# Two block sizes from one gram of 96 columns, and a unit's VectorE work cut into pieces, in a woven RWKV6 and Mixer kernel

## Chip, cores and metric

One core of one Trainium2 chip. The metric is the device time in microseconds (us) of that core. Ratios are taken between runs of the same rounds on the same chip. Engines are written as the profile writes them: PE is TensorE's products, PEld its weight loads, DVE is VectorE, ACT is ScalarE, POOL is GpSimd. The words "issue" and "releaser" are the profile's: the releaser is what ended an idle stretch, and "issue" means that the engine waited for nothing that the profile shows.

## The reference

```python
B, H, S, D = 4, 8, 768, 48                 # batch, heads, tokens, head dim
state = zeros(B, H, D, D)
for t in range(S):                         # the recurrence, "attention" below
    cur = einsum('bhd,bhe->bhde', u * k[t], v[t])
    y[t] = einsum('bhd,bhde->bhe', r[t], state + cur)
    state = w[t][..., None] * state + einsum('bhd,bhe->bhde', k[t], v[t])
x = y as (B, S, H * D)                     # 384 wide
h = relu(x.T @ w_tok1) @ w_tok2            # token mixing, 256 wide
u = x + h.T
out = u + relu(u @ w_ch1) @ w_ch2          # channel mixing, 1536 wide
```

The kernel does the recurrence in chunks of 64 tokens. Within a chunk the weights of token on token are built up in levels: level l joins blocks of b = 2^l tokens in pairs, and needs the *gram* (the products of k with r) of each right block with its left one, multiplied by the decay between. A *unit* is 256 tokens of a batch with all heads: three units to a batch, twelve in all.

## The kernel before

PE is kept busy by mixing: while batch n is mixed, the three units of batch n + 1 are computed in between. `woven` decides what stands where: each list of pieces is spread evenly by the weights of its pieces, and the lists are merged. A weight is thus not a time that anything checks, only a share of the list.

```python
def woven(*lists):
    keyed = []
    for n, pieces in enumerate(lists):
        total, at = sum(c for c, _ in pieces), 0.0
        for i, (c, f) in enumerate(pieces):
            keyed.append(((at + c / 2) / total, n, i, c, f))
            at += c
    return [(c, f) for *_, c, f in sorted(keyed, key=lambda e: e[:3])]
```

The levels of a unit. A gram goes through four 64-row tiles of the array side by side (`fours`); a join is one or two multiplications on VectorE that bring r, k and the decays from one level to the next; a pick copies what is valid of a gram into the unit's weights, under a mask. From unit 6 on (`NEAR`) level 0 is not a gram but row sums on VectorE (`nearest`).

```python
def gram(l):                                   # level 1 to 4, one block size each
    b = 1 << l
    right = r_.rearrange("p (n two b) -> p n two b", two=2, b=b)[:, :, 1, :]
    g = L["g"] = ps_g.tile([128, 2, 512], f32, name="gram")
    for ca in range(UC * A):
        fours(lambda q, j, rows, cols: pe.matmul(
            g[cols, q, ts(ca, 32)], k_[rows, ds(ca * 128 + j * T, T)],
            right[rows, ts(2 * ca + j, 32 // b), :], start=True, stop=True))
...
def join(l, w, new):
    ...
    dve.tensor_mul(halves, halves, by)                           # r and k, 1024 elements a row
    dve.tensor_mul(new[:ROWS], wv[:, :, 0], wv[:, :, 1])         # the decays of the next level

def block(l):
    gram(l)
    join(l, products[l], products[l + 1])
    pick(l)
...
pieces = [(0.1, begin)] + ([(1.6, first_block)] if i < NEAR else [])
for l in range(1, LEVELS):
    pieces.append((1.2, lambda l=l: block(l)))
```

`beside` puts the end of one unit (`tokens`, `carry`, `update`, `before`, `within`: products with the state and the values) and the levels of the next unit into one list; `one` ties two groups of small products together, so that they come one behind the other. The last lines weave that list with the mixing of a batch. The z products (`up`) and q products (`down`) are the mixing's full-size ones; `turned` is the second half of token mixing with the transposes behind it.

```python
def beside(i, after, ahead):
    tokens, carry, update, before, within, *loads = after
    begin, *rest = ahead
    row0, row1, place = nearest(i + 1)
    ...
    return [(1.0, begin[1]), tokens, one(carry, rest[0]), update, one(before, rest[1]), one(within, rest[2]),
            *loads, *rest[3:], row0, row1, place]
...
for bt in range(B):
    ...
        hiddens, pieces, ups, downs = mixing(bt)
        pieces = [(3.9, lambda h=h: emit(h)) for h in hiddens] + pieces
        for s in range(S // SEG):
            pieces += ups[s] + downs[s]
    ...
        for i in range(n, n + UB):
            att += beside(i, post(i), levels(i + 1)) if i + 1 < NU else post(i)
        emit(woven(att, pieces))
```

## Time and profile before

| | before |
|---|---|
| time, median of 3 runs | 604.68 us (603.76 to 605.39) |
| span in the profile | 601.6 us |
| PE, PEld, DVE, ACT busy | 570.0, 486.6, 361.0, 177.1 us |
| loop: batch 0 mixed, units 3 to 5 between, from 138.5 us | 90.4 us, PE idle 3.5 |
| batch 1 mixed, units 6 to 8 between | 134.6 us, PE idle 0.3 |
| batch 2 mixed, units 9 to 11 between | 129.7 us, PE idle 0.05 |
| batch 3 mixed, nothing between | 105.2 us, PE idle 0 |

The lower four rows cut the span. ("The loop" is the first of these.) Where PE and PEld overlap, PE idle is the length less PE's busy time.

### The profile page before, as it was taken

Reading aid. Unit: us, or ns where it says so; the run is one execution under the profiler, and the core shown is the slowest. Engines: PE = TensorE matmul, PEld = TensorE weight load, DVE = VectorE, ACT = ScalarE, POOL = GpSimd, SP = SyncE. Lnnn points to the kernel's source line nnn. Section 1 sums busy time; section 2 is a strip of 40 time slices with the busy share of each in tenths; the row PEclk is TensorE's granted clock in tenths of the full one; section 3 lists DMA queues with packets and bytes.
Section 4 is the critical chain, followed back from the end, with each engine's and each line's share of the span. In section 5 each row is a group of like instructions: output and inputs, shape, how many; then the busy total and the mean of one; then the engine's idle time right before and its main releaser. Section 6 shows DMA issues by size and latency. Waiting matters only on the chain.

```text
span 601.6 us, 18874 instructions
## 1 busy us (share of the span) xinstructions
PE 570.0 (95%) x8596; PEld 486.6 (81%) x8596; DVE 361.0 (60%) x599; ACT 177.1 (29%) x428; POOL 7.2 (1%) x32
## 2 busy tenths in 40 slices
PE   3787899899999989999999999999999999999997
PEld 2776658776888886789989896789898986898987
DVE  5789699999675867666457376528446422040404
ACT  6155444422433313241141231231313312302020
POOL 4000000000000000000000000000000000000000
PEclk9997599999999999999999999999999999999999
DMA  8534564620233235141124103001200000000000
GB/s 340 195 83 152 163 199 151 208 70 28 82 110 109 67 82 158 29 133 28 53 57 132 28 28 106 2 2 43 65 2 28 2 27 0 1 20 8 27 2 27
DMA packets 22976, 45.85 MB, mean 76 GB/s; under 512 B 2512, under 2 KB 14928, under 8 KB 22896
## 3 DMA queue, kind: packets, MB, share of 16 engines
q1 hardware_dynamic: 22752, 44.64, 23.3%
q8 instruction: 67, 1.10, 0.8%
q14 instruction: 13, 0.11, 0.1%
q10 hardware_dynamic: 144, 0.00, 0.0%
HBM read 39.91 MB, written 4.72 MB: 74 GB/s over the span
## 4 chain that ended last, share of the span: by engine, by line
PE 79%; DVE 13%; DMA 3%; issue 3%; ACT 2%; SPq 0%; DVEq 0%; ACTq 0%
PE z_ps L554 29%; PE q_ps L588 24%; PE gram L307 7%; PE h_ps L534 4%; PE h_ps L527 4%; DVE rk L341 3%; DMA x<-in_w_ch_dram 2%; PE h_ps L564 2%; PE kv_ps L440 2%; PE y_ps L489 2%; PE y_ps L476 2%; PE gram L430 2%; DVE at L323 2%; PE xT_ps L546 1%; DVE scratch L218 1%
## 5 line engine op out<-in xcount | busy, mean ns | idle before, releaser
L554 PE MATMUL z_ps<-xT,wch 128*128 128x256 f32 x864 | 195.9, 382 | 1.6 <-ACT z L556 1.6
L554 PEld LDWEIGHTS z_ps<-xT,wch 128*128 128x128 f32 x864 | 161.0, 190 | 23.8 <-ACT z L556 2.8
L556 ACT ACTIVATE z<-z_ps 128x256 f32<-128x256 f32 x144 | 55.0, 382 | 171.3 <-PE z_ps L554 158.2
L588 PE MATMUL q_ps<-wch,z 128*128 128x192 f32 x528 | 94.6, 329 | 0.0
L588 PEld LDWEIGHTS q_ps<-wch,z 128*128 128x128 f32 x528 | 86.1, 190 | 1.4
L588 PE MATMUL q_ps<-scratch,z 128*128 128x192 f32 x396 | 70.0, 328 | 0.0
L307 PE MATMUL gram<-rk 48*64 48x32 f32 x3072 | 62.7, 234 | 6.6 <-issue 3.2
L307 PEld LDWEIGHTS gram<-rk 48*64 48x64 f32 x3072 | 58.2, 152 | 12.4 <-issue 6.4
L341 DVE TENSOR_TENSOR rk<-rk,decay 112x1024 f32<-112x1024 f32 x36 | 44.0, 1223 | 35.7 <-PE gram L307 26.1
L588 PEld LDWEIGHTS q_ps<-scratch,z 128*128 128x128 f32 x396 | 64.4, 190 | 0.4
L341 DVE TENSOR_TENSOR rk<-rk,w 112x1024 f32<-112x1024 f32 x36 | 44.0, 1223 | 28.9 <-PE gram L307 23.9
L580 DVE TENSOR_TENSOR z<-z 128x768 f32<-128x768 f32 x11 | 10.5, 957 | 65.6 <-ACT z L556 65.6
L527 PE MATMUL h_ps<-x,wtok 128*128 128x384 f32 x96 | 35.6, 518 | 0.0
L534 PE MATMUL h_ps<-h,wtok 128*128 128x384 f32 x96 | 35.3, 492 | 0.0
L323 DVE COPY_PREDICATED at<-mask,gram 128x512 f32<-128x512 uint8 x36 | 32.2, 895 | 0.0
L457 DVE TENSOR_TENSOR state<-state,kv_ps 128x192 f32<-128x192 f32 x40 | 14.2, 356 | 24.4 <-PE kv_ps L440 23.5
L331 ACT COPY at<-gram 16x256 f32<-16x256 f32 x48 | 17.4, 363 | 33.7 <-PE gram L307 32.5
L536 DVE TENSOR_TENSOR x<-x,h_ps 128x384 f32<-128x384 f32 x24 | 13.3, 553 | 23.1 <-PE h_ps L534 23.1
L527 PEld LDWEIGHTS h_ps<-x,wtok 128*128 128x128 f32 x96 | 18.5, 201 | 10.4 <-issue 0.6
L534 PEld LDWEIGHTS h_ps<-h,wtok 128*128 128x128 f32 x96 | 16.4, 190 | 9.6 <-ACT h L529 2.6
L431 ACT COPY kT<-gram 128x512 f32<-128x512 f32 x24 | 14.0, 585 | 28.5 <-PE gram L430 28.3
L318 ACT COPY at<-gram 32x256 f32<-32x256 f32 x48 | 17.4, 363 | 14.2 <-PE gram L301 13.7
(84 smaller groups left out, 514.9 us busy)
## 6 DMA issues: line engine op xcount, KB each, us to landing
rk<-in_rkw_dram SPq DMA_DIRECT2D x36, 192.0 KB, 3.4
x<-in_w_ch_dram SPq DMA_DIRECT2D x10, 512.0 KB, 4.3
vt<-in_v_dram SPq DMA_DIRECT2D x12, 384.0 KB, 4.4
out_dram<-o SPq DMA_DIRECT2D x24, 192.0 KB, 1.9
rp<-in_near_dram SPq DMA_DIRECT2D x12, 384.0 KB, 3.6
scratch<-in_w_ch_dram SPq DMA_DIRECT2D x8, 512.0 KB, 4.3
w<-in_rkw_dram SPq DMA_DIRECT2D x18, 192.0 KB, 3.2
rk<-in_rkw_dram SPq DMA_DIRECT2D x6, 512.0 KB, 6.5
```

What stands on the lines that cost most here:

```text
L307: fours(lambda q, j, rows, cols: pe.matmul(g[cols, q, ts(ca, 32)], k_[rows, ds(ca * 128 + j * T, T)], right[rows, ts(2 * ca + j, 32 // b), ...
L318: act.copy(at[p:p + b, :, ts(c, A), b:], g[ds(p + c * b, b)])
L323: dve.copy_predicated(out=dst, data=g.rearrange("p q (m b) -> p q m b", b=b), mask=masks[l].rearrange("p x t -> p (x t)").rearrange("p (m ...
L331: act.copy(at[p:p + b, :, :, n * 2 * b + b:(n + 1) * 2 * b], g[p:p + b, :, :, ts(n, b)])
L341: dve.tensor_mul(halves, halves, by)
L431: act.copy(L["kT"][:, c], ps)
L457: dve.tensor_add(new, new, got)
L527: pe.matmul(sums[i], wtok1[:, c, ts(i, 128)], xs[bt][:, c, :], start=(c == 0), stop=(c == C - 1))
L534: pe.matmul(ps, wtok2[:, i, ts(c, 128)], h1[:, i, :], start=(i == 0), stop=(i == DTOK // 128 - 1))
L554: pe.matmul(ps, wch1[:, m, ts(jt, 128)], xT[:, m, ts(s, SEG)], start=(m == 0), stop=(m == DM // 128 - 1))
L556: act.activation(zs[s][:, jt, :], ps, AF.Relu)
L588: pe.matmul(ps, a[:, j, :], b[:, j, :], start=(j == 0), stop=(j == HJ - 1))
```

## The change

The intent: from batch 2's units on (unit 6 and later) two levels share one gram. Each group of four blocks b needs six block columns: the right neighbour of a pair (level l) and, for level l + 1, the r of blocks 2 and 3 brought forward past blocks 1 and 2. Those 32 + 64 = 96 columns are laid out first (`spread`), one gram of 96 columns replaces two of 32, and three picks of 3b, 2b and b columns take it apart. VectorE pays with more and smaller operations. Because these would hold up the mixing's own VectorE work, they become pieces of their own, with weights of their own.

```diff
+        def spread(l, c):
+            ...
+            late(newest(act), act, copies)                       # two copies on ScalarE
+            dve.tensor_mul(y[:, :, 1:5:3], of[:, :, 2:4], ...)
+            dve.tensor_mul(y[:, :, 2], y[:, :, 4], ...)
+        def gram4(l):
+            for c in range(UC):
+                g = L["g", c] = ps_g.tile([128, 2, 512], f32, name="gram")
+                for a in range(A):
+                    fours(lambda q, j, rows, cols: pe.matmul(
+                        g[cols, q, ts(a, 96)], k_[rows, ds((c * A + a) * 128 + j * T, T)],
+                        L["far", c][rows, ts(2 * a + j, 96)], start=True, stop=True))
+        ... join_k, join_r, pick4 (three predicated copies a half unit)
+        if i >= NEAR:
+            return pieces + [(c, lambda f=f, a=a: f(*a)) for l in (1, 3) for c, f, a in (
+                (0.9, spread, (l, 0)), (0.9, spread, (l, 1)), (1.5, gram4, (l,)), (1.5, join_k, (l,)), (1.5, join_r, (l,)),
+                (1.4, pick4, (l, 0)), (1.4, pick4, (l, 1)))] + [(0.9, lambda: block(5))]
...
-        return [(0.3, lambda c=c: late(newest(dve), dve, lambda: row(c))) for c in range(UC)] + [
-            (0.2, lambda: (place(), load_near(i + 1)))]
+        return [(x, lambda c=c, n=n: late(newest(dve), dve, lambda: row(c, n)))
+                for c in range(UC) for n, x in enumerate((1.0, 0.6, 1.0))] + [(2.0, place)]
...
+        return [(2.0, begin[1]), far0, far1, tokens, one(carry, gram), join_k, join_r, loads[2], later0, pick0, loads[3], later1,
+                pick1, one(before, gram_), join_k_, join_r_, (0.01, lambda: load_near(i + 1)), pick0_, pick1_,
+                one(within, last), *loads[:2], *ends]
```

(`loads[2]` and `loads[3]` are the two halves of the state's update.) The list of a near unit now weighs 34.2 where it weighed 12.2, while the lists of earlier units keep their weights.

## The prediction

> **What bounds the kernel now.** I read the page's slices first, then busy time by stretch, then the groups, then TensorE's timeline around a few groups. The slices show who is full.
>
> ```profile
> PE   3787899899999989999999999999999999999997
> PEld 2776658776888886789989896789898986898987
> DVE  5789699999675867666457376528446422040404
> ```
>
> From the tenth slice on TensorE (PE) is at 9 nearly everywhere, while VectorE (DVE) falls from 9 to between 2 and 7. A busy PE alone proves little, so I cut the span at the starts of the three later batches (the first token-mixing products of L527, at 228.86, 363.44 and 493.10 us in the chain of waits) and at the start of the loop that mixes batch 0 with the attention of batch 1 (138.5 us).
>
> ```profile
> 138.50:228.86 90.36, 86.89 (x2294) 75.68 (x2294) 66.31 (x114) 29.59 (x77) 0.33 (x3) 1.00 0.28 82
> 228.86:363.44 134.58, 134.24 (x2064) 116.66 (x2063) 84.92 (x148) 36.50 (x92) 0.22 (x2) 1.00 0.24 71
> 363.44:493.10 129.66, 129.61 (x1743) 112.12 (x1743) 66.65 (x123) 32.47 (x81) 0.00 (x0) 1.00 0.10 31
> 493.10:598.34 105.24, 105.23 (x534) 92.42 (x533) 24.54 (x45) 18.60 (x47) 0.00 (x0) 1.00 0.03 10
> ```
>
> Columns: stretch, length, then busy us of PE, PEld, DVE, ACT, POOL, granted clock, DMA. The last batch is mixing alone, 105.2 us. Batch 1 has the same mixing plus three units of attention: 134.6 - 105.2 = 29.4 us. A unit's own products are tokens 0.9, carry, before and within 0.97 each, five grams 4.85 (below), together some 8.7 us, and 0.2 us lost at each return to full-size products makes it 9.7; three units are 29. So that stretch is the sum of its products: **no wait is left in it to win, only product time.** The same holds for batch 2 (two units' levels, three units' ends). Only the loop before, 138.5 to 228.86, has idle: 90.36 - 86.89 = 3.5 us plus about 2 us of slow stretches inside busy groups.
>
> The part that the change touches is the grams:
>
> ```profile
> L307 PE MATMUL gram<-rk 48*64 48x32 f32 x3072 | 62.7, 234 | 6.6 <-issue 3.2
> L341 DVE TENSOR_TENSOR rk<-rk,decay 112x1024 f32<-112x1024 f32 x36 | 44.0, 1223 | 35.7 <-PE gram L307 26.1
> L323 DVE COPY_PREDICATED at<-mask,gram 128x512 f32<-128x512 uint8 x36 | 32.2, 895 | 0.0
> ```
>
> 3072 records are 12 units x 4 levels x 32 products x 2 records. The mean of 234 ns is latency; the rate comes from the timeline, start to start:
>
> ```profile
> 293.70 1.10 PE L307 MATMUL gram<-rk 48*64 48x32 f32 x64
> 294.73 6.74 PE L554 MATMUL z_ps<-xT,wch 128*128 128x256 f32 x30
> 301.40 1.15 PE L489 MATMUL y_ps<-vt,at 64*64 64x48 f32 x64
> 302.37 1.10 PE L307 MATMUL gram<-rk 48*64 48x32 f32 x64
> 303.40 5.45 PE L554 MATMUL z_ps<-xT,wch 128*128 128x256 f32 x24
> 308.78 1.14 PE L307 MATMUL gram<-rk 48*64 48x32 f32 x64
> ```
>
> A level of 32 columns takes 1.03 us behind a group of the same tiling (302.37 to 303.40), 1.06 alone; 64 records of 48 columns take 0.97 (301.40 to 302.37). So 15 to 16.6 ns a record, whatever the columns. In the timeline the 64-column gram of the earlier units (L284) also takes 1.06. The z products run at 215.8 ns a record (15.54 us for 72 in the last batch's chain), so 30 should take 6.47 and take 6.67: 0.2 us goes at each return from small tiles.
>
> **What the Trainium skill says.** "TensorEngine Tiling (Array Packing)", Instruction Overhead, says that a product of 1 column has the latency of one of 60. The trace agrees in kind: 32, 48 and 64 columns cost the same. Key Properties there says that changing the tiling mode drains the array; the 0.2 us agrees in kind. "VectorE: DVE Perf Modes", the errata section, gives (N+151)/0.96 ns for a float32 tensor-tensor operation; the trace has 354 ns at 192, 553 at 384, 953 at 768 and 1223 at 1024, which is the same line to 1%, so I use it (via the trace) for sizes not seen. "Perfetto Trace Analysis", Identifying the Most-Contended Engine, warns that matmul occupancy overstates; hence the sum above.
>
> **The change part by part**, for units 6 to 11 (six of twelve).
>
> TensorE. Now, levels 1 to 5: 1.04 + 1.03 + 1.03 + 1.06 + 0.69 = 4.85 us a unit. After: two grams of 64 records with 96 columns stand for levels 1 to 4, and level 5 stays (0.69). The full array needs 215.8/256 = 0.84 ns a column, so 96 columns stream in 81 ns; four tiles side by side make 20.2 ns a record. At 64 columns that bound is 13.5 and 16.5 was seen, so the bound begins to bind between; I take 21.5 ns (an estimate), 1.38 us a gram. Then 2 x 1.38 + 0.69 = 3.45, **1.40 less.** Small groups: before carry, before and within each carry a gram, and levels 4 and 5 stand alone (five returns); after there are three returns. Two fewer, some 0.15 to 0.2 each: 0.3. Sum 1.7 us a unit, **10.2 us in six.** All is on the path, since batches 1 and 2 are sums of products; only unit 6, in the loop before, is less sure.
>
> VectorE. Now a unit's joins are 6 x 1.223 + 1.97 (decay products, 0.68 + 0.42 + 0.29 + 0.22 + 0.18 + 0.17) = 9.30 and its picks 1.29 + 0.70 + 0.70 = 2.69 (the 1.29 is level 1, runs of two): 12.0. After: join 0, 1.91; four spreads of 256 and 128 elements, 4 x (0.42 + 0.29) = 2.84; k joins 1.53 and 1.33; r joins 1.40 and 1.30; twelve predicated copies of 384, 256, 128 elements at 0.085 + 1.2 ns an element (from 0.70 at 512 and 1.31 at 1024), 1.18 per half unit, with a surcharge for short runs at level 1, together 5.4 (estimate); last join 1.40. Sum 17.1: **5.1 more a unit, 31 in all**, VectorE from 361 to about 392 us. ScalarE loses four copies of 0.363 (level 4) and gets eight of about 0.4 to 0.45: 2 us more a unit. All this lies beside TensorE: batch 1's VectorE goes from 85 to about 100 of some 129 us, the loop before from 66 to 72 of some 89.
>
> Order. The new piece weights (34 a unit instead of 12) squeeze units 3 to 5 into the first half of the loop before (33.7 of 67.9, formerly 33.7 of 46), and unit 11's end into the last 6% of batch 2. The first makes the join-gram chain of those units tighter, perhaps 2 us of new waits, though batch 1's first products are then free to fill in early; the second costs under 1 us, as each piece still has a product of 1.95 us behind it. Splitting updates and row sums costs nothing and lets additions of q products in between. Building the masks is a few small operations once.
>
> Sum: 604.7 - 10.2 + about 2 (loop before, net) + about 0.5 (VectorE in batches 1 and 2, mostly hidden) - 0.5 (two returns unit 6 or waits in its grams saved) = **596.5 us**, 1.4% less.
>
> **Rivals.** (1) VectorE becomes the bound in the quarter-product stretches. There mixing alone takes 6.7 of 13.65 us of VectorE, and attention adds about 10 of what is then some 17 us: full. Each q product needs an addition before its accumulator is free. Against it: in the stretches of z products there is no mixing work on VectorE, and finer pieces were made for just this. If it holds, 1 us is lost in each of some six such stretches and the pace of the loop before slips: 601 to 606. (2) The four tiles don't stream 96 columns side by side, say two share a path: 40 ns a record, 2.6 us a gram, the gain gone: 605 to 608. Against it: 64 columns at 16.5 ns would then be 27. (3) Both gram buffers are held from the gram to the picks, some 7 to 10 us, just where batches 1 and 2 turn their activations through the same buffers: up to 2 us each, 598 to 601. Against: the token-mixing back products need no such buffer. (4) The looser order also removes the 5 us of waits in the loop before: 590 to 592.
>
> **Range and chances.** The product term is 8 to 11 us; the waits between -4 and +7. Hence 591 to 602.5 in 8 of 10. The 2% line is 592.6, which needs full product gain and rival 4: 0.15. Slower than 616.8 needs rivals 1 and 2 together: 0.03. Within 2%: 0.82.
>
> **What would show it.** Right: 96-column gram groups of 64 records in 1.3 to 1.45 us start to start; 768 of them in all; 32-column records of L307 halved to 1536; batch 1 about 129.5 us and batch 2 about 126; VectorE 385 to 397 us busy; three returns a unit. Wrong: PE idle in batch 1 above 2 us with VectorE additions or gram buffers as the releaser (rivals 1, 3), 25 ns or more a record (rival 2), or the loop before longer than 90 us.

## The result, and the profile after

| | before | after |
|---|---|---|
| median of 6 runs each | 603.88 us (602.67 to 605.39) | 610.77 us (608.01 to 615.58) |
| ratio of the fast runs, 95% interval | | 1.0118 (1.0078 to 1.0158) |
| span in the profile | 601.6 | 609.0 |
| loop, PE idle | 90.2, 3.5 | 101.1, 8.2 |
| batch 1, PE idle | 134.6, 0.3 | 133.2, 2.5 |
| batch 2, PE idle | 129.7, 0.05 | 128.6, 1.8 |

A ratio here and below is the mean time of one kernel's fast runs over the mean of the other's fast runs of the same rounds, so it is not quite the ratio of the medians quoted. The change costs 1.2%: within 2% of before, yet well outside the range that was predicted, and on the wrong side. (The stage lengths are cut at the first product of each stage in the trace, hence 90.2 for the loop before where the prediction's window has 90.4.)

The slices after. PE has an 8 in slices 11, 13 and 15 where it had 9, and the granted clock (PEclk, tenths of full speed) drops to 7 and 8 in slices 12 and 13:

```profile
PE   3787799999898989999999999999999999999997
DVE  5789699999764798876639677727584351040403
PEclk9999699999978999999999999999999999999999
```

The stages (columns as in the prediction: stretch, length, busy us of PE, PEld, DVE, ACT, POOL, clock, DMA):

```profile
137.31:238.43 101.12, 92.92 (x2169) 80.51 (x2169) 75.44 (x143) 31.04 (x83) 2.70 (x17) 0.93 0.26 75
238.43:371.61 133.18, 130.72 (x1680) 113.15 (x1679) 96.09 (x213) 37.64 (x101) 0.22 (x2) 1.00 0.25 71
371.61:500.22 128.61, 126.84 (x1489) 109.69 (x1487) 73.06 (x161) 32.26 (x86) 0.00 (x0) 1.00 0.09 29
```

The loop got 10.9 us longer, at a mean clock of 0.93. Batches 1 and 2 each got a little over a microsecond shorter: PE's busy time there fell by 3.5 and 2.8 us, but idle time that was not there before took 2.1 and 1.7 of it back. The groups of the grams (L308 here is the line that is L307 in before):

```profile
L308 PE MATMUL gram<-rk 48*64 48x32 f32 x1536 | 38.4, 257 | 8.8 <-issue 5.7
...
L410 DVE COPY_PREDICATED at<-mask,gram 128x384 f32<-128x384 uint8 (+2 forms) x72 | 34.5, 482 | 14.4 <-PE gram L384 13.7
```

As many grams as predicted have gone: 1536 records of 32 columns remain (and 768 of 96 columns stand for the rest). From start to start in the trace, 64 of the new records take 1.45 us, 22.7 ns a record. In batch 1 the grams' time from start to start fell from 12.60 to 8.71 us. VectorE is at 386.2 us.

So where did the loop's 10.9 us go? PE's timeline in its middle, before, and after. (Columns: start us, busy us, engine, line, operation, tiles, count of records, and in brackets the idle time ahead with its releaser. A product of the program makes two records; the counts of products that are read from traces below are records.)

```profile
189.31 1.13 PE L307 MATMUL gram<-rk 48*64 48x32 f32 x64
190.37 2.86 PE L554 MATMUL z_ps<-xT,wch 128*128 128x256 f32 x12
193.16 1.15 PE L489 MATMUL y_ps<-vt,at 64*64 64x48 f32 x64
194.13 1.10 PE L307 MATMUL gram<-rk 48*64 48x32 f32 x64
```

```profile
188.98 1.15 PE L561 MATMUL y_ps<-state,rk 48*64 48x48 f32 x64 [0.45 <-DVE state L542]
189.92 0.88 PE L308 MATMUL gram<-rk 48*64 48x32 f32 x45
192.79 0.74 PE L308 MATMUL gram<-rk 48*64 48x32 f32 x18 [1.99 <-issue]
193.25 0.32 PE L574 MATMUL y_ps<-vt,at 64*64 64x48 f32 x2
```

In the kernel before, twelve full-size products (2.8 us) stand between two pairs of small groups. After, nothing does: state products, gram, value products and gram follow one another, 256 small products in a row, and after 109 of them PE stands still for 1.99 us with no releaser that the profile shows. The same happens at 166.32 us (1.50 us). The waits of PE in the loop (us in total, times, longest):

```profile
PE gram L308 <- issue: 3.5, 2, 2.0
PE q_ps L674 <- DVE o L688: 2.1, 1, 2.1
PE y_ps L561 <- DVE state L542: 1.2, 2, 0.8
```

Behind each of the two stops the granted clock is half for 6.8 us (168.9 to 175.75 and 192.8 to 199.6). That half clock costs more than the stop: where PE is the bound, 6.8 us at half speed do 3.4 us of work (an estimate; a gram of 64 products at half clock, from 170.56 us, took 1.86 us instead of 1.06). The sum for the loop: 4.7 us more idle, 2 x 3.4 from the clock, less some 1.5 that unit 6's new grams save, +10.0 of the +10.9 seen. (Before, no half clock falls in the loop. Both kernels have some ahead of it: before from 54.0 to 74.5 us, after from 66.5 to 76.8.)

Why a stop with no releaser? The trace records the fetches of instructions, as packets of 16,384 bytes. Before, the page counts 67 of them with 1.10 MB, and after, 61 with 1.00 MB. PE and PEld records times 64 bytes give 17,192 x 64 = 1.10 MB and 15,656 x 64 = 1.00 MB. So nearly all these packets are TensorE's, at 64 bytes an instruction: one packet holds 256 instructions, 128 pairs of weight load and product. At 16.5 ns a small product it lasts 2.1 us. The stop at 166.32 us ended 1.3 us after a packet had come in at 166.5 us, that at 190.80 us 1.7 us after one at 191.06. "Runtime: NRT & Kernel Launch", Instruction fetch mechanics, of the Trainium skill describes such fetches (blocks of 16 KiB, 256 instructions) and calls the cost of crossing a block "mostly hidden". The theory, then: **a long run of small products uses instructions up faster than they come.** It had to be tested, as "issue" only says what the profile does not show.

### The profile page after: what moved, and what is told of

It is laid out like the page before. It is cut to its first block, busy times and chain, and to the rows that moved or that the text cites. A ratio compares the mean times of both kernels' runs of the same rounds, so it can differ in the third digit from the quotient of the medians.

```text
span 609.0 us, 17474 instructions
## 1 busy us (share of the span) xinstructions
PE 568.1 (93%) x7828; PEld 484.6 (80%) x7828; DVE 386.2 (63%) x729; ACT 180.9 (30%) x452; POOL 9.6 (2%) x46
## 4 chain that ended last, share of the span: by engine, by line
PE 76%; DVE 14%; issue 4%; ACT 3%; DMA 2%; SPq 0%; DVEq 0%; ACTq 0%
PE z_ps L640 26%; PE q_ps L674 22%; PE h_ps L613 5%; PE h_ps L620 4%; PE gram L308 4%; PE kv_ps L522 2%; PE y_ps L574 2%; PE y_ps L561 2%; PE gram L512 2%; DVE at L410 2%; DVE rk L342 2%; PE h_ps L650 2%; PE xT_ps L632 1%; PE gram L384 1%; DVE state L542 1%
## 5 line engine op out<-in xcount | busy, mean ns | idle before, releaser
L674 PE MATMUL q_ps<-wch,z 128*128 128x192 f32 x528 | 94.6, 330 | 0.2 <-DVE z L700 0.2
L674 PEld LDWEIGHTS q_ps<-wch,z 128*128 128x128 f32 x528 | 87.6, 192 | 1.4 <-DVE z L700 0.5
L674 PE MATMUL q_ps<-scratch,z 128*128 128x192 f32 x396 | 71.9, 334 | 2.9 <-DVE o L688 2.9
L674 PEld LDWEIGHTS q_ps<-scratch,z 128*128 128x128 f32 x396 | 65.4, 193 | 4.2 <-DVE o L688 3.5
L308 PE MATMUL gram<-rk 48*64 48x32 f32 x1536 | 38.4, 257 | 8.8 <-issue 5.7
L308 PEld LDWEIGHTS gram<-rk 48*64 48x64 f32 x1536 | 35.7, 178 | 13.5 <-issue 6.7
L342 DVE TENSOR_TENSOR rk<-rk,decay 112x1024 f32<-112x1024 f32 x24 | 29.4, 1223 | 24.9 <-PE gram L302 15.5
L410 DVE COPY_PREDICATED at<-mask,gram 128x384 f32<-128x384 uint8 (+2 forms) x72 | 34.5, 482 | 14.4 <-PE gram L384 13.7
L342 DVE TENSOR_TENSOR rk<-rk,w 112x1024 f32<-112x1024 f32 x24 | 29.4, 1225 | 9.7 <-PE gram L308 7.4
L613 PEld LDWEIGHTS h_ps<-x,wtok 128*128 128x128 f32 x96 | 18.4, 199 | 10.9 <-issue 0.6
L622 DVE TENSOR_TENSOR x<-x,h_ps 128x384 f32<-128x384 f32 x24 | 13.3, 555 | 20.9 <-PE h_ps L620 20.9
L542 DVE TENSOR_TENSOR state<-state,kv_ps 128x192 f32<-128x192 f32 x40 | 14.1, 352 | 18.0 <-PE kv_ps L522 17.2
L633 ACT COPY xT<-xT_ps 128x384 f32<-128x384 f32 x24 | 11.5, 478 | 35.6 <-PE xT_ps L632 35.6
L512 PE MATMUL gram<-ident,rk 128*128 128x128 f32 x96 | 17.6, 311 | 3.8 <-ACT kT L513 3.1
```

Of the source, the lines that this page charges most:

```text
L308: fours(lambda q, j, rows, cols: pe.matmul(g[cols, q, ts(ca, 32)], k_[rows, ds(ca * 128 + j * T, T)], right[rows, ts(2 * ca + j, 32 // b), ...
L410: dve.copy_predicated(out=to[:, :, :, (q + 1) * b:], data=got[:, :, :, first * b:first * b + n], mask=masks4[l][:, q].unsqueeze(1).unsquee ...
L512: pe.transpose(ps[:, a, :], k_[:, ts(c * A + a, 128)], ident)
L542: dve.tensor_add(new, new, got)
L613: pe.matmul(sums[i], wtok1[:, c, ts(i, 128)], xs[bt][:, c, :], start=(c == 0), stop=(c == C - 1))
L622: dve.tensor_add(x[:, c, :], x[:, c, :], ps)
```

## The experiments

Three questions: what lengthens the loop, where the saving in batches 1 and 2 went, and whether both can be had. The theories at the start, in words: that the *order* made by the new weights (small products bunched, so that instructions run out and the clock falls) costs the loop's 10.9 us; against it, that *VectorE's added work* fills it (the prediction's first rival), or that the *grain of the pieces* does.

### e1_weights: the old weight for the new list

```diff
-        return [(2.0, begin[1]), far0, far1, tokens, ...]
+        near = [(2.0, begin[1]), far0, far1, tokens, ...]
+        return [(c * 0.36, f) for c, f in near]
```

The list weighs 12.3, close to the 12.2 of before the change; the work is that of after, to the instruction.

> The changed kernel with one edit: every weight of a near unit's list times 0.36, so that the list weighs 12.3 as before and units 3 to 5 are spread over the loop before batch 1 as in the kernel before. Theory A (the weave squeezed units 3 to 5, two groups of 256 small records came without a mixing product between, TensorE stood still there and its clock then fell to half): no half clock after 77 us, the loop from 137 us to batch 1's first L613 product falls from 101 to 89-91 us, the whole to 598-602. Rival B (VectorE's extra work in unit 6 and after is what costs): the loop stays above 97 us and the whole above 607. The rest (batches 1 and 2) should stay within 1 us of 133 and 128.5 us by both.

Measured 603.33 us against 604.47 for before, ratio 0.9988 (0.9966 to 1.0010).

```profile
139.90:230.40 90.50, 86.75 (x2165) 75.61 (x2165) 72.42 (x140) 31.45 (x83) 2.69 (x17) 0.98 0.31 84
230.40:363.60 133.20, 130.73 (x1680) 113.17 (x1679) 97.23 (x215) 37.70 (x101) 0.22 (x2) 1.00 0.25 71
```

The loop is back at 90.5 us from 101.1, with idle 3.8 instead of 8.2, and the half clock is down to one stretch of 3.4 us (behind a stop in unit 6's second gram, see e9). VectorE does the same work. So the loop's loss is the weights'. Batch 1 is as after, 133.2: its waits have another cause.

### e2_before_heavy: the new weight in the kernel before

```diff
-        return [(1.0, begin[1]), tokens, ...]
+        pieces = [(1.0, begin[1]), tokens, ...]
+        return [(c * (2.78 if i + 1 >= NEAR else 1.0), f) for c, f in pieces]
```

> The kernel before with one edit: the weights of the lists that hold a near unit's levels times 2.78, so that units 3 to 5 are squeezed as in the changed kernel, but every gram, join and pick is the old one. Theory A: the same two groups of 256 small records, gaps of 1.5 us or more in them, two stretches at half clock near 169 and 193 us, the loop from 138 us to batch 1 grows from 90 to 97-101 us, the whole to 610-614. Rival B (the new VectorE work is the cause): 603-606, no half clock after 75 us.

Measured 616.81 us, ratio 1.0184 (1.0144 to 1.0225).

```profile
138.30:242.00 103.70, 95.63 (x2298) 83.18 (x2298) 71.69 (x119) 30.56 (x79) 0.34 (x3) 0.92 0.28 78
```

```profile
PE gram L307 <- issue: 6.0, 4, 2.0
```

The loop takes 103.7 us with none of the change's work in it: only the weight differs. Four stops with "issue" as the releaser, of 1.49, 1.99, 0.65 and 1.92 us, and behind three of them half clock of 3.4, 6.8 and 6.8 us. Together with e1 this settles the first question: the order does it, in either kernel, and the grams of 96 columns are not needed for it.

### e4_coarse: two-size grams in coarse pieces with the old weights

```diff
+        def group(weight, *pieces):
+            return (weight, lambda: [f() for _, f in pieces])
+        return [(1.0, begin[1]), group(0.6, far0, far1), tokens, (2.3, one(carry, gram)[1]), group(1.2, join_k, join_r, pick0, pick1), ...]
```

> The changed kernel with the pieces joined again (k join, r join and both picks as one; both updates as one; row sums as two) and the old list weights, so the two-size gram alone, without the fine pieces. If the fine pieces are what keeps VectorE out of the way of the q products, this is 3-8 us slower than the changed kernel with its weights scaled (602-608); if the pieces' size matters little, it is within 2 us of it (597-603).

Measured 607.09 us, ratio 1.0037 (1.0010 to 1.0064). Loop 91.8, batches 1 and 2 together 261.5 us, where e1 with fine pieces has 261.9. So in batches 1 and 2 the grain makes no difference. The whole time is another matter: it is 3.8 us above e1's, which is the 602 to 608 expected if the fine pieces matter. The profiled run, the fastest of the four (604.46 us), had one stop of 1.95 us at 166.63 us in the loop and half clock behind it; the other three (607.03 to 607.62) have no profile. The list also weighs 13.4 here by its pieces, not 12.2. Whether the many small pieces, the second part of the change's idea, buy anything in the loop is therefore not shown.

### e3_dense and e11_wide: a run of small products by itself

Into the last batch, which has no attention, 16 extra grams whose results nobody uses: eight back to back (512 products), eight singly, each between pieces of six z products.

```diff
+                if bt == B - 1 and s == 1:
+                    more = ups[s][:6] + [(0.01, lambda: [small() for _ in range(8)])] + ups[s][6:]
+                if bt == B - 1 and s == 2:
+                    more = [e for f in ups[s] for e in (f, (0.01, small))][:16] + ups[s][8:]
```

> The kernel before plus 16 gram groups (64 records each, results unused) in the last batch, where nothing but TensorE limits: eight of them in one piece of 512 records, eight each behind three z products. Their operands are long ready and no reader waits. If fetching instructions limits dense small products (rival to a wait on VectorE), the 512 records show gaps of 0.5-2 us each ended by no engine, near the landings of instruction packets, and take 10-16 us instead of 8.5, while the spaced groups show none; perhaps half clock follows. If the gaps in the changed kernel came from VectorE alone, the 512 records take 8.3-8.6 us.

Correct, 629.14 us. The dense run:

```profile
547.88 2.99 PE L647 MATMUL gram<-rk 48*64 48x32 f32 x189
552.32 2.07 PE L647 MATMUL gram<-rk 48*64 48x32 f32 x128 [1.45 <-issue]
556.07 5.88 PE L647 MATMUL gram<-rk 48*64 48x32 f32 x195 [1.68 <-issue]
561.87 1.65 PE L554 MATMUL z_ps<-xT,wch 128*128 128x256 f32 x3
```

No reader waits and the operands are long ready, and yet PE stops after 189 products, and again after exactly 128 more, one packet's worth. The packets of instructions began to come at 549.93, 553.39, 557.45 and 561.52 us, 3.5 to 4.1 us apart, and each was in some 1 us later. Other transfers cannot have held them up much: the DMA engines were 2% busy. 512 products took 13.99 us instead of the 8.5 that eight single grams (1.06 us each, no stop) add up to, and the clock was half from 554.3 to 564.5 us, so that the last 195 took 30 ns each without a stop. Still it could have been the tiles, or having no reader. So e11 runs the same count with 192 columns, which stream more slowly:

```diff
-                pe.matmul(g[ts(j, T), q, ts(ca, 32)], k_[...], r_[rows, ds(ca * 128 + j * T, 32)],
+                pe.matmul(g[ts(j, T), q, ts(ca % 2, 192)], k_[...], r_[rows, ds(ca // 2 * 192, 192)],
```

> The same 16 added groups as in e3, each record with 192 instead of 32 columns: as many instructions, but 40 ns or more of streaming a record, so a packet of 256 instructions lasts some 5 us instead of 2. If it is the supply of instructions that fails in dense small products, the 512 records now run without gaps of 0.5 us or more (in e3 two of 1.5 and 1.7 us), in 20.5-23 us, and at full clock. If small tiles themselves, or the missing reader, stop TensorE, the gaps stay.

```profile
548.78 21.03 PE L647 MATMUL gram<-rk 48*64 48x192 f32 x512
569.74 2.42 PE L554 MATMUL z_ps<-xT,wch 128*128 128x256 f32 x10
```

Again one look, correct, 649.27 us. 512 products in one piece, 20.96 us (40.9 ns each), full clock, no stop; the packets came 4.8 to 5.4 us apart, as they were used up. Same tiles, same count, no readers: it is the rate of instructions that stops PE. Shown: the supply keeps up with a product in 40.9 ns and not with one in 16.5. Where between them it gives out was not measured; in all fifteen traces no two of these packets begin less than 3.3 us apart, which for 128 products is 26 ns each (an estimate). In the nine stops of this kind of 1.4 us and more (after, e2, e3, e4, e8), PE went on 2.4 to 2.9 us after a packet began to come, where 128 small products last 2.1 us. How long a run may be before it stops is not one number: 189 products here, 109 in the kernel after.

### e7_few_picks: VectorE relieved, with a wrong result

The second question. In batches 1 and 2 PE now stands idle with VectorE as the releaser. The waits of PE in batch 1 of the kernel after:

```profile
PE xT_ps L632 <- DVE x L622: 0.8, 1, 0.8
PE q_ps L674 <- DVE o L688: 0.8, 1, 0.8
PE z_ps L640 <- DVE o L712: 0.4, 1, 0.4
PE xT_ps L632 <- DVE at L410: 0.3, 1, 0.3
```

Either VectorE has too much to do, or the mixing's additions (L622, L688, L712) stand behind the wrong things in its queue. Dropping two of three predicated copies tells these apart.

```diff
-            for q, first in enumerate((0, 3, 5)):
+            for q, first in enumerate((0,)):
```

> e1 with two of the three predicated copies of each pick left out: a wrong result on purpose. The order on TensorE is that of e1; VectorE loses 4 x (0.43 + 0.43) = 3.4 us a unit and is near the load of the kernel before. Theory C: TensorE's waits in batches 1 and 2 fall from 2.4 and 1.2 us to under 1 and 0.6, batch 1 to 130.5-132 us, batch 2 to 127-128, the whole to 599-601.5. If VectorE's added work doesn't matter, all stays within 0.5 us of e1 (603).

Measured 600.52 us, ratio 0.9942 (0.9903 to 0.9980), result wrong as meant.

```profile
226.80:360.10 133.30, 130.87 (x1679) 113.36 (x1679) 91.98 (x192) 37.74 (x101) 0.22 (x2) 1.00 0.25 71
```

VectorE does 5.2 us less in batch 1 (91.98 against e1's 97.23), and batch 1 takes 133.3 us against 133.2, batch 2 128.5 against 128.7. So the amount of work is not what makes batches 1 and 2 wait, as far as this cut reaches: 91.98 us is still above the 84.9 of before. This went against the expectation that load was the cause. The time gained lies in the loop (88.7 against 90.5), where a stop of 1.26 us and the half clock of e1 are gone (see e9).

### e5_sparse_q, e6_sparse_qt: attention kept away from the mixing's VectorE stretches

If the place in the queue is the cause, e1's own queue must show it. VectorE ahead of the addition that PE's transposes wait for:

```profile
240.36 0.36 DVE L539 COPY state<-kv_ps 128x192 f32<-128x192 f32 x1 [1.27 <-PE kv_ps L522]
...
243.50 0.95 DVE L393 TENSOR_TENSOR rk<-rk,decay 112x768 f32<-112x768 f32 x1
244.37 0.41 DVE L410 COPY_PREDICATED at<-mask,gram 128x128 f32<-128x128 uint8 x1
244.60 0.57 DVE L622 TENSOR_TENSOR x<-x,h_ps 128x384 f32<-128x384 f32 x1
```

VectorE itself stood idle for 1.27 us until the carry's products were there, then ran 4.2 us of attention work, and only then came L622; PE had waited 0.82 us for it. VectorE takes its pieces in the order of its queue here, so a piece that waits for PE holds up all behind it. The cure is another weave: give the mixing's pieces a smaller weight where they need VectorE, and fewer attention pieces fall there.

```diff
+            pieces = pieces[:len(hiddens)] + [(c * 0.4, f) for c, f in pieces[len(hiddens):]]   # e6 only
             for s in range(S // SEG):
-                pieces += ups[s] + downs[s]
+                pieces += ups[s] + [(c * 0.4, f) for c, f in downs[s]]                           # e5 and e6
```

> e1 with one more edit: in batches 1 to 3 each q-product piece counts 0.4 of its weight when pieces are woven, so fewer attention pieces fall among the q products, where VectorE has its mixing work. Theory C (what is lost in batches 1 and 2 is TensorE waiting for VectorE's mixing additions and for gram buffers behind bursts of attention work): waits for the q additions go, batch 1 falls from 133.2 to 130-132 us, batch 2 from 128.7 to 127-128, the whole to 600-602. Rival D (the loss is in the turned part, or is spread whatever the weave): 602-605.

> e5 with the back products and the turns counted 0.4 as well. Theory C: the waits of the turns for VectorE's additions to x and for gram buffers go too, batch 1 129.5-131.5 us, batch 2 126-127.5, the whole 598-601. Rival D: 602-605.

e5 is inconclusive. Its fast runs (604.95, 605.76, 607.85 us) have a ratio of 1.0033 (0.9986 to 1.0080), but the profiled run was slow: 950.04 us, with a granted clock of 0.56 from 77 us almost to the end, so there is no profile to compare. e6 measured 604.19 us, ratio 0.9995 (0.9953 to 1.0036). Batch 1 went to 132.0, batch 2 to 130.1: the waits had moved, now 1.5 us at one q product of batch 2 (L674, for the addition L688), not gone. By the whole time both runs fall where rival D was expected (e5 even above it).

### e8_both: e6, with more weight for unit 6's list

```diff
-        return [(c * 0.36, f) for c, f in near]
+        return [(c * (0.36 if i >= NEAR else 0.42), f) for c, f in near]
```

> e6 with the list of unit 6 alone (loop before batch 1) at 0.42 instead of 0.36, chosen because the order on TensorE then has six or more mixing products between any two gram-and-y groups of units 3 to 5 and eight before unit 6's second one. If dense small products are what costs in that loop, it falls from 90.5 to 87-89 us and the whole to 596-599; if it is the chain of joins, it stays at 90 or more and the whole equals e6.

A miss: 608.11 us, ratio 1.0064 (1.0013 to 1.0115), the loop 95.0 instead of 87 to 89, with two stops: 1.92 us at 166.96 us without a releaser and 3.4 us of half clock behind it, and 1.97 us at 218.94 us, a wait for the state (L542), with 6.8 us. Moving the lists against each other moves the small groups, and whether PE stops depends on more than the mixing between them. In this trace no packet began between 159.55 and 166.34 us, and PE stood until 168.88. Where the packets' boundaries fall seems to matter; that has not been tested by itself.

### e9_turned: e1, with attention kept off the whole of token mixing

```diff
             pieces = [(3.9, lambda h=h: emit(h)) for h in hiddens] + pieces
+            pieces = [(c * 0.05, f) for c, f in pieces]
```

Here only the token-mixing pieces of batches 1 to 3 get less, but nearly all of it, the first half (`hiddens`) included.

> e1 with one more edit: in batches 1 to 3 the token-mixing pieces (L613, L620 and the turns) count 0.05 of their weight, so that attention begins only after the turned part, which then runs as in the last batch, with nothing of attention ahead of its additions to x in VectorE's queue. Theory F (in batches 1 and 2 TensorE waits because the order in VectorE's queue puts attention pieces ahead of a mixing addition, not because of VectorE's load): the waits of the turns (0.8 us and its slow products, once or twice a batch) go, batch 1 falls from 133.2 to 131.5-132.5, batch 2 from 128.7 to 127.5-128.3, if the denser pieces after it bring no new wait; the whole 601-603. Load theory: the sum stays at 261-263 us, since the same work is packed into less time.

Measured 599.90 us, ratio 0.9940 (0.9912 to 0.9968), correct.

```profile
231.50:361.10 129.60, 129.60 (x1680) 112.87 (x1679) 97.80 (x213) 36.99 (x101) 0.22 (x2) 1.00 0.25 72
```

Batch 1 is 129.6 us, PE without a gap, with as much work on VectorE as in e1 (97.80 against 97.23). e7 and e9 together settle the second question: **the order of the pieces cost batch 1 its 3.6 us, not VectorE's load.** (The weave orders all engines; that it acts through VectorE's queue is read from e1's lines above.) Batch 2 is 128.6, with 1.6 us of idle left. The loop had 6.8 us of half clock from 219.0 us, and the stops around it were waits for VectorE: 0.95 us for the state (L542), then 1.26 us within unit 6's second gram.

```profile
219.42 0.42 DVE L410 COPY_PREDICATED at<-mask,gram 128x128 f32<-128x128 uint8 x1
219.98 1.56 PE L384 MATMUL gram<-rp,rk 48*64 48x96 f32 x32 [1.26 <-DVE w L391]
```

The page names L391, but this gram reads nothing of it. There are two gram buffers, and the last of the earlier level's three picks of this half unit, which frees the one needed, ended 0.14 us before the gram went on. The same 1.26 or 1.27 us stand in the loops of e1, e6 and e10, each time 0.14 to 0.15 us after that pick and with half clock around or behind it. In e7, which leaves out that pick and keeps PE's order, the gram waited 0.22 us and the loop had no half clock. So the prediction's third rival, the gram buffers, is at work there.

### e10_turned_prio: e9, with priority for the mixing's VectorE operations

```diff
+        def first(op, *a, **k):
+            with tc.high_priority(offset=60) if bt else nullcontext():
+                op(*a, **k)
...
-            dve.tensor_add(x[:, c, :], x[:, c, :], ps)
+            first(dve.tensor_add, x[:, c, :], x[:, c, :], ps)      # and so for all of them
```

> e9 with the mixing's VectorE instructions of batches 1 to 3 at higher priority for the scheduler, so that they come ahead of the row sums and joins wherever both are ready; the order on TensorE is that of e9. Theory F: 0.5-1.5 us less than e9 in batches 1 and 2 together, the whole 600-602. If the order doesn't matter: as e9.

Measured 601.46 us, ratio 0.9960 (0.9938 to 0.9981). Loop, batch 1 and batch 2 take 90.8, 129.7 and 128.7 us, close to e9's 91.7, 129.6 and 128.6; the loop merely starts later (142.3 us), with an extra stretch of half clock ahead of it. The hint to the scheduler changes nothing that can be seen here.

### e12_before_turned: the new weave in the kernel before, as a control

```diff
             pieces = [(3.9, lambda h=h: emit(h)) for h in hiddens] + pieces
+            pieces = [(c * 0.05, f) for c, f in pieces]
```

> The kernel before with e9's second edit alone (token-mixing pieces of batches 1 to 3 at 0.05 of their weight), a control for e9: is its gain the grams' or the weave's? If the grams': batches 1 and 2 stay within 1.5 us of 134.6 and 129.7, the whole at 602-605. If the weave's: they fall by 3 us or more and the whole to 599-601.

Measured 605.75 us, ratio 1.0012 (0.9990 to 1.0035); batches 1 and 2 take 134.6 and 130.0 us. The weave alone gives nothing: what e9 gains in batch 1 is product time of the change, let through.

### e13_spaced: both cures

e9, and unit 6's list spaced by its products instead of its VectorE work: its row sums weigh next to nothing, the rest fills the 12.3.

```diff
+        if i < NEAR:
+            return [(c * 0.455, f) for c, f in near[:-len(ends)]] + [(c * 0.01, f) for c, f in ends]
         return [(c * 0.36, f) for c, f in near]
```

> e9 with the row sums of unit 6 at weight 0.01 and the rest of its list at 0.455, so that nine q products instead of three lie between its two groups of kv or y products and 96-column grams, and all else in TensorE's order is that of e9. If the dense products cause the stop near 216-220 us (gaps of 0.9 and 1.2 us, then half clock), the gap in the gram and the half clock go, the loop falls from 91.7 to 87.5-89.5 us, the whole to 596-599. If the kv-update chain or the addition L688 causes it, a gap of about 1 us stays and the whole is 599-601.

Measured 596.74 us (595.08 to 597.96) against 605.07 for before, ratio 0.9867 (0.9841 to 0.9893), correct. It beats both kernels, 1.3% under before.

```profile
138.30:226.00 87.70, 84.79 (x2166) 73.89 (x2165) 69.58 (x138) 29.13 (x78) 3.42 (x17) 1.00 0.29 80
226.00:355.80 129.80, 129.80 (x1684) 113.06 (x1679) 100.34 (x216) 39.33 (x107) 0.23 (x2) 1.00 0.27 76
355.80:484.30 128.50, 127.07 (x1489) 109.90 (x1488) 73.58 (x162) 33.73 (x89) 0.00 (x0) 1.00 0.09 30
```

Full clock in the whole loop, no stop of 1 us or more. The outcome is neither of the two that were expected: the half clock went, but a gap of 0.87 us in the second gram stayed, and here the page itself names the pick (L410) as its releaser. What the spacing did was to put products of mixing where PE had waited for the state (0.95 us in e9, nothing here) and to shorten the wait for the buffer. Against before: loop -2.5, batch 1 -4.8, batch 2 -1.2 us, and the span -8.6.

## Why the prediction was wrong

Predicted 596.5 (591 to 602.5), measured 610.8. By its own steps:

**The bound: right.** Batches 1 and 2 were sums of their products before, and e9 shows it once more: with the order put right, batch 1 takes 129.6 us, where the prediction's product sum gave 129.5.

**The grams: right in rate.** 22.7 ns a record where 21.5 was estimated, 1.45 us a gram of 64 where 1.38 was. Per unit the grams saved (12.60 - 8.71) / 3 = 1.3 us where 1.40 was forecast. The returns to full-size products in batch 1 fell from 15 to 9, five to three a unit, as forecast. With the waits gone (e9) batch 1 is 134.6 - 129.6 = 5.0 us shorter, 1.7 a unit in all, as predicted. The rival of tiles that share a path (40 ns) is refuted.

**VectorE's size: right.** +25.2 us (386.2) where "385 to 397" was named and 31 worked out; the predicated copies 34.5 / 6 = 5.75 us a unit where 5.4 was. (Its reading of the slices, VectorE "between 2 and 7" after the tenth, is loose: the line runs from 8 down to 0.)

**"About 2 (loop before, net)": the step that failed.** It measured +10.9. The prediction saw that the weights press the earlier units into the first half of the loop, and called this "perhaps 2 us of new waits". For waits on data that was about right: in the loop they rose from 1.6 to 4.5 us, 2.1 of it in one wait (L674, for L688). What it missed is what dense runs of small products do by themselves: two stops of 1.5 and 2.0 us for lack of instructions and, the larger term, 6.8 us of half clock behind each, worth some 6.8 us together. The profile of before held a hint: "issue" as the main releaser ahead of L307, 3.2 us in all, in the very line quoted. The prediction does not ask where it came from. In the loop of the kernel before, two stops of 0.7 us carry that releaser. e1 and e2 show that the weight alone turns this on and off.

**"About 0.5 (VectorE in batches 1 and 2, mostly hidden)": failed as well, smaller.** It was 133.2 - 129.6 = 3.6 us in batch 1. For batch 2 no version without waits exists; PE's idle time there went from 0.05 to 1.8 us. The step reasoned from totals (some 100 of 129 us busy) and was right that the load fits, as e7 and e9 show; wrong in taking that for "hidden". The load can fit and the order still be bad. So its first rival named the right engine ("VectorE becomes the bound in the quarter-product stretches") with the wrong mechanism: less load did not help, another order did. The third rival, the gram buffers, was there too: PE waited 0.3 us in batch 1 and 1.2 us in batch 2 for picks (L410) to free a buffer for transposes, and, with the old weight, 1.3 us in the loop, with half clock (e9). Its sign of being wrong, over 2 us of idle in batch 1 with VectorE as the releaser, came true (2.5 us).

**Batch 2 "about 126": not reached by any version.** 128.1 us in the best (e4, 0.75 of it idle), 128.5 in e13, of which 1.4 is idle. Without that idle time e13 saves 2.6 of the 3.4 us that two units' levels were to save.

That e13's 596.74 equals the 596.5 predicted is partly chance: its loop gained 2.5 us where the prediction had it about even, and batch 2 gave less. **Open** are why at a given spacing a stop falls or does not (e8; packet boundaries are the guess), why half clock follows some stops and not others (a wait of 2.1 us at 226.45 us in the loop of after, among full-size products, was followed by none), what is left in batch 2, and e5. Also the loop starts between 137.3 and 142.3 us in kernels whose code up to there is nearly alike, which is why stages were compared and not only totals.

## What to carry to other kernels

Small products are cheap on the array and dear in instructions: keep full-size products between groups of them, and read "issue" ahead of a tiled group, with the granted clock right behind it, as a sign of instructions running short; half clock by itself is none, since it followed waits for VectorE too (e9). When work is woven by weights, a list's total weight is part of the schedule of every *other* list in the weave; change it only on purpose. And an engine with room to spare still makes others wait if its queue holds a piece that waits in front of a piece that is waited for: look at the queue just ahead of the releaser, not at its busy share.

## What the Trainium skill lacked or had wrong

- "Runtime: NRT & Kernel Launch", Instruction fetch mechanics, calls the crossing of a 16 KiB block of instructions mostly hidden. Here 512 dense products of 32 columns took 13.99 us instead of 8.5 and PE stopped for 1.45 and 1.68 us (e3); with 192 columns there was no stop (e11). That section gives PE 2048 instructions of room; the first stop came after 189 products, 378 instructions, and the next after exactly 256 more. A rate at which the supply gives out is missing: here no two packets of 256 began less than 3.3 us apart, and PE went on 2.4 to 2.9 us after one began.
- "TensorE: Matmul & The Clock Gate", Why this matters for your kernels, has the clock fall after idle gaps of about 3 us. Here single stops of 1.3 to 2.0 us, among small products, were followed by half clock (in the kernel after two of them by 6.8 us each), while one of 2.1 us among full-size products was not. The stretches behind the stops lasted mostly 3.4 or 6.8 us, one or two of the windows that the page describes; the 10.2 us of e3 are three. A caveat there tells of 50 us stuck at a low clock; one run here was at a granted clock of 0.56 from 77 us to 948 us (e5).
- The same page, "Wait — 56ns, not 53.3ns?", gives about 25 ns as the least time from the start of one product to that of the next. That does not hold for tiles side by side: with four of them, 64 products of 48 columns took 0.97 us, 15.2 ns each.
- "TensorEngine Tiling (Array Packing)" has no figure for the drain on a change of tiling: about 0.2 us a return here. Nor has it a rate for four tiles of 64 rows side by side: 16.5 ns a product at 32 columns, 22.7 at 96, 40.9 at 192.
- None of the pages gives a time for a predicated copy: 0.70 us at 512 elements in runs of four and more, 1.29 in runs of two; 0.48 us mean over 384, 256 and 128.
